# Scatters and gathers from 128 partitions, route steps at two a position late in an item, and register reads item by item

## The chip, the cores and the metric

The kernel runs on one core of a Trainium2 chip. The core has a matrix engine (TensorE, PE in the rows), three engines for elementwise work (VectorE, DVE; ScalarE, ACT; GpSimd, POOL) and a sync engine (SP) that here only issues transfers and reads values into its registers. Each engine takes its instructions in the order of its own program and waits in place for what an instruction needs. The metric is the time of one execution in microseconds, less is better. Before the change the median of three timed runs is 1078.88 us (1070.05 to 1081.38).

## What is computed

Attention with a decaying state, then two layers of experts. The first layer sends a token to one expert, the second to two of eight.

```python
x = attn(q, k, v, a_re, a_im)                  # 3072 tokens x 384
e_idx = argmax(x @ w_gate + modality_bias)     # layer 1: one expert of 8
out[mask] = gate_w * (relu(x[mask] @ w1[e]) @ w2[e])
noisy = x @ w_gate + log1p(exp(x @ w_noise)) * noise
top2 = argpartition(-noisy, 2)[:, :2]          # layer 2: two experts of 8
out[mask] += top2_w * (relu(x[mask] @ w1[e]) @ w2[e])
```

## The kernel before

Attention runs first, by a planner's order, and writes its rows `x1` to HBM. Both expert layers then work in *items*. An item is one block of a token list for one expert: 3 blocks of 122 tokens in layer 1 (`CUT1`; items 6 and 9 are small, one block), 4 blocks of 99 in layer 2 (`CUT2`). Layer 1 has 10 items that always run, layer 2 has 16; more run only behind a branch (`singles`) that tests a count, and in this execution none of them did.

An item (`experts`) is 8 groups of 9 matmuls into `ph` and 3 groups of 24 into `po`, each product in three passes for precision (high by high, high by low, low by high). After each of these 11 groups there is a *position*, p = 0 to 10, at which side work is written into the program: splits of the next item's weights (`w1h`, `w1l` at 7, 7, 8; `w2h`, `w2l` at 0, 2, 3, 5), transposes of the next item's gathered rows `xg` into `xh`, `xl` (`turn`, at 8, 8, 9), the rest of the item before (`fin`, at 0 to 3), and one step of the *route*.

The route (`route2`) turns the noise gates of two or three finished layer-1 items into entries of the second list. It is a generator of nine steps: six of a chain of small VectorE operations up to the mask `mbf`, one in which nothing is done, one in which PE counts ranks (`pr`, matmuls of `ones` and `before` with `pb` and `mbf`; the tile shows as `pt`) and VectorE starts on the slots, and one that ends the `slot` and issues 12 or 14 scatters of `ent` into `list2` on POOL, one for each block and choice. It is set going at p = 3, so that its steps stand at p = 4 to 10 and then at p = 0 and 1 of the next item. There are four routes: in items 2, 4 and 7 of layer 1, and in item 0 of layer 2.

For the second layer, `lead_blocks` loads three list blocks (`lt0` to `lt2`) on POOL's queue once the third route's scatters have landed; `gather2` then gathers the rows `x2` into `xg`, and `prior2` gathers what `out` holds so far into `op`; `out` is scattered back at an item's end (`out_dram<-og`). Weights are loaded into a ring of four buffers `raw` on SP's queue (`load1`, `load2`). Expert numbers and list positions lie in a table (`tb`, or `tbl` for the first three), and the engine that issues a transfer reads them with a value load (TENSOR_LOAD). `load1` and `load2` each read the expert, `block` reads the position. A scheduler places instructions as early as their inputs allow, so value loads come together where a table is ready.

## Time and profile before

| | |
|---|---|
| median of three timed runs | 1078.88 us |
| time of the profiled execution | 1068.24 us |
| its span, first to last instruction | 1066.6 us |
| PE busy | 952.2 us, 89% |
| DVE, ACT, POOL busy | 684.9, 543.3, 550.9 us |
| mean granted TensorE clock | 0.96 of full |

The page gives the busy time of each engine, and the span in 40 slices. A timeline row is a start, a duration, the engine, the line and the operation with its tiles, written `out<-in`; in brackets stands how long the engine was idle before it, and the name of what ended the wait. Most instructions are recorded by one helper and so have its line (L394); they are told apart by tiles. Attention takes the first 308 us, layer 1 runs to 572 us, layer 2 to the end.

### The profile page before, as it was taken

Reading aid. Unit: us, or ns where it says so; the run is one execution under the profiler, and the core shown is the slowest. Engines: PE = TensorE matmul, PEld = TensorE weight load, DVE = VectorE, ACT = ScalarE, POOL = GpSimd, SP = SyncE. Lnnn points to the kernel's source line nnn. Section 1 sums busy time; section 2 is a strip of 40 time slices with the busy share of each in tenths; the row PEclk is TensorE's granted clock in tenths of the full one; section 3 lists DMA queues with packets and bytes.
Section 4 is the critical chain, followed back from the end, with each engine's and each line's share of the span. In section 5 each row is a group of like instructions: output and inputs, shape, how many; then the busy total and the mean of one; then the engine's idle time right before and its main releaser. Section 6 shows DMA issues by size and latency. Waiting matters only on the chain.

```text
span 1066.6 us, 18507 instructions
## 1 busy us (share of the span) xinstructions
PE 952.2 (89%) x6330; PEld 902.7 (85%) x6330; DVE 684.9 (64%) x1504; ACT 543.3 (51%) x990; POOL 550.9 (52%) x449
## 2 busy tenths in 40 slices
PE   2597979889899999999967898899999999999993
PEld 1476767778789999999957798899999999999993
DVE  7599999888767585858844663555555555555540
ACT  7587768777354454456543242444444444444430
POOL 4475766565544237281466386555555444445331
PEclk9898999999999999999987898999999999999997
DMA  6475766531464656577575255665555555565420
GB/s 163 119 202 131 191 177 153 130 118 39 127 166 126 191 150 146 155 188 204 132 179 156 52 99 169 214 186 168 172 166 176 181 177 174 181 186 178 138 75 26
DMA packets 119340, 161.55 MB, mean 151 GB/s; under 512 B 39820, under 2 KB 102091, under 8 KB 119226
## 3 DMA queue, kind: packets, MB, share of 16 engines
q1 hardware_dynamic: 95258, 126.57, 40.4%
q0 software_dynamic: 23968, 33.61, 12.7%
q8 instruction: 54, 0.88, 0.4%
q14 instruction: 60, 0.49, 0.2%
HBM read 130.13 MB, written 30.71 MB: 151 GB/s over the span
## 4 chain that ended last, share of the span: by engine, by line
PE 58%; DVE 11%; issue 10%; DMA 8%; SPq 4%; POOL 4%; ACT 3%; POOLq 0%; DVEq 0%; ACTq 0%
PE po L394 24%; PE ph L394 23%; PE pt L394 5%; SPq L394 2%; POOL list L836 2%; DMA xg<-x,lt 2%; DMA im<-in_a_im_dram 1%; DMA list<-ent,slot 1%; DMA raw<-in_moe_w_dram 1%; PE pp L394 1%; DVE S L394 1%; PE py L394 1%; DVE im L394 1%; PE ptr L394 1%; PE pc L394 1%
## 5 line engine op out<-in xcount | busy, mean ns | idle before, releaser
L394 PE MATMUL ph<-xh,w1h 128*128 128x396 f32 (+1 forms) x576 | 204.7, 355 | 8.9 <-DVE og L869 4.5
L437 POOL DMA_INDIRECT xg<-x,lt x90 | 118.7, 1319 | 175.5 <-DMA lt<-list 64.2
L394 PE MATMUL po<-hh,w2h 128*128 128x396 f32 (+1 forms) x576 | 199.8, 347 | 5.1 <-ACT oT L608 5.1
L394 PE MATMUL ph<-xl,w1h 128*128 128x396 f32 (+1 forms) x576 | 196.7, 342 | 0.0
L394 PE MATMUL ph<-xh,w1l 128*128 128x396 f32 (+1 forms) x576 | 196.2, 341 | 0.0
L394 PE MATMUL po<-hh,w2l 128*128 128x396 f32 (+1 forms) x576 | 196.1, 341 | 0.0
L394 PE MATMUL po<-hl,w2h 128*128 128x396 f32 (+1 forms) x576 | 195.7, 340 | 0.0
L593 ACT ACTIVATE hh<-ph 128x396 fp32r<-128x396 f32 (+1 forms) x192 | 94.5, 493 | 167.6 <-PE ph L394 145.1
L595 DVE SCALAR_TENSOR_TENSOR hl<-ph,hh 128x396 fp32r<-128x396 f32 (+1 forms) x192 | 107.3, 559 | 59.8 <-ACT hh L593 54.7
L608 ACT ACTIVATE oT<-po 128x396 f32<-128x396 f32 (+1 forms) x72 | 35.4, 492 | 175.4 <-PE po L394 166.0
L437 POOL DMA_INDIRECT op<-out_dram,lt x64 | 87.3, 1364 | 72.5 <-DMA out_dram<-og,lt 52.1
L836 POOL DMA_INDIRECT list<-ent,slot x52 | 95.9, 1845 | 47.2 <-DVE slot L833 30.4
L394 PEld LDWEIGHTS ph<-xh,w1h 128*128 128x128 f32 x576 | 109.9, 191 | 10.4 <-DVE og L869 4.8
L873 POOL DMA_INDIRECT out_dram<-og,lt x64 | 68.8, 1076 | 93.5 <-DVE og L869 63.6
L394 PEld LDWEIGHTS po<-hh,w2h 128*128 128x128 f32 x576 | 109.0, 189 | 5.6 <-ACT oT L608 5.5
L556 DVE TENSOR_TENSOR w1l<-raw,w1h 128x1024 fp32r<-128x1024 f32 x78 | 92.2, 1218 | 28.6 <-ACT w1h L556 26.6
L394 PEld LDWEIGHTS ph<-xl,w1h 128*128 128x128 f32 x576 | 110.3, 191 | 0.0
L394 PEld LDWEIGHTS ph<-xh,w1l 128*128 128x128 f32 x576 | 109.9, 191 | 0.1
L394 PEld LDWEIGHTS po<-hl,w2h 128*128 128x128 f32 x576 | 109.3, 190 | 0.0
L394 PEld LDWEIGHTS po<-hh,w2l 128*128 128x128 f32 x576 | 108.8, 189 | 0.0
L869 DVE SCALAR_TENSOR_TENSOR og<-pt,lt,op 99x384 f32<-99x384 f32 x64 | 39.1, 617 | 107.7 <-PE pt L394 71.4
L556 DVE TENSOR_TENSOR w2l<-raw,w2h 128x768 fp32r<-128x768 f32 x104 | 98.9, 951 | 11.0 <-ACT w2h L556 9.3
(341 smaller groups left out, 1810.8 us busy)
## 6 DMA issues: line engine op xcount, KB each, us to landing
raw<-in_moe_w_dram SPq DMA_DIRECT2D x78, 512.0 KB
raw<-in_moe_w_dram SPq DMA_DIRECT2D x104, 384.0 KB
x<-zero SPq DMA_DIRECT2D x12, 457.5 KB
re<-in_a_re_dram SPq DMA_DIRECT2D x24, 192.0 KB
q<-in_q_dram SPq DMA_DIRECT2D x24, 192.0 KB
im<-in_a_im_dram SPq DMA_DIRECT2D x24, 192.0 KB
k<-in_k_dram SPq DMA_DIRECT2D x24, 192.0 KB
v<-in_v_dram SPq DMA_DIRECT2D x24, 192.0 KB
```

The source lines that it names most:

```text
L394: o = f(*a, **kw)
L437: nc.gpsimd.indirect_dma_start(out=dst, out_offset=None, in_=src, in_offset=bass.IndirectOffsetOnAxis(ap=idx, axis=0), bounds_check=n - 1, ...
L556: a, b = nc.scalar.activation(h, r, AF.Copy), nc.vector.tensor_sub(l_, r, h.bitcast(FT))
L593: relu = nc.scalar.activation(a, p, AF.Relu)
L595: rest = nc.vector.scalar_tensor_tensor(l, p, 0.0, a.bitcast(FT), op0=OP.max, op1=OP.subtract)
L608: nc.scalar.activation(oT[:, d, :], p, AF.Copy)
L836: nc.gpsimd.indirect_dma_start(out=list2_v[2 * b + j], out_offset=bass.IndirectOffsetOnAxis(ap=slot[:, j, b:b + 1], axis=0), in_=ent[:, j, ...
L869: nc.vector.scalar_tensor_tensor(og[:, b, :], p, gate[:, b:b + 1], opv[:, b, :], op0=OP.mult, op1=OP.add)
L873: nc.gpsimd.indirect_dma_start(out=out_v[b], out_offset=bass.IndirectOffsetOnAxis(ap=lt[:, b, 1:2], axis=0), in_=og[:, b, :], in_offset=No ...
```

## The change

Tiles that POOL scatters from or gathers into get 128 partitions in place of 122, with the last six set once at the start: `lts`, `lt1s` and `slots` to an index out of bounds, `ents` to zero. The scatters of the second list and the gathers of layer 1 then name all 128 partitions. `new_side` puts two route steps at p = 8, 9 and 10. An expert number is read once for an item, and value loads on SP are queued behind the last `w1` load issued before them.

```diff
-    xgs = [consts.tile([TB_, NB_, XW], FT, name=f"xg{i}") for i in range(2)]
-    lts = [consts.tile([TB_, NB_, 4], I32, name=f"lt{i}") for i in range(K)]
+    xgs = [consts.tile([128, NB_, XW], FT, name=f"xg{i}") for i in range(2)]
+    lts = [consts.tile([128, NB_, 4], I32, name=f"lt{i}") for i in range(K)]
+    lt1s = [consts.tile([128, CUT1.NB, 3], I32, name=f"lu{i}") for i in range(4)]
+    slots = [consts.tile([128, 2, MR], I32, name=f"slot2{i}") for i in range(3)]
+    ents = [consts.tile([128, 2, MR, 4], I32, name=f"ent2{i}") for i in range(3)]
+    for t_ in lts + lt1s + slots:
+        nc.gpsimd.memset(t_, BIG)
+    for t_ in ents:
+        nc.gpsimd.memset(t_, 0)
...
+    def read(x, n, q_=nc.sync):
+        if q_ is nc.sync and loaded and any(i is loaded[-1] for i in nc.cur_bb.bb.instructions):
+            with tc.issue_after(loaded[-1]):
+                return q_.value_load(x, min_val=0, max_val=n)
+        return q_.value_load(x, min_val=0, max_val=n)
+    loaded = []
+
     def block(lt, r, l, cut, q_=nc.sync):
-        r = q_.value_load(r, min_val=0, max_val=(E + 1) * cut.CAP - cut.T)
+        r = read(r, (E + 1) * cut.CAP - cut.T, q_)
...
     def load1(e, w1_):
-        e = nc.sync.value_load(e, min_val=0, max_val=E - 1)
...
-            nc.sync.dma_start(r, w1_[bass.ds(e, 1), d * 128:(d + 1) * 128, :].rearrange("o p f -> p (o f)"))
+            a = nc.sync.dma_start(r, w1_[bass.ds(e, 1), d * 128:(d + 1) * 128, :].rearrange("o p f -> p (o f)"))
             split(side, r, wts[0][:, d, :], wts[1][:, d, :])
+        loaded[:] = [a.ins]
...
     def load2(e, w2_):
-        e = nc.sync.value_load(e, min_val=0, max_val=E - 1)
...
-        e = (first or tb[1])[:, 0, i:i + 1]
+        e = read((first or tb[1])[:, 0, i:i + 1], E - 1)
...
-                gather(xg[:cut.TB, b, :], x1, lt[:cut.TB, b, 0:1], N)
+                gather(xg[:, b, :], x1, lt[:, b, 0:1], N)
...
-        ahead1[i] = wk.tile([CUT1.TB, CUT1.NB, 3], I32, name="lt1", bufs=6)
+        ahead1[i] = lt1s[i % len(lt1s)]
...
-                    out=list2_v[2 * b + j], out_offset=bass.IndirectOffsetOnAxis(ap=slot[:, j, b:b + 1], axis=0),
-                    in_=ent[:, j, b, :], in_offset=None, bounds_check=E * CUT2.CAP - 1, oob_is_err=False)
+                    out=list2_v[2 * b + j], out_offset=bass.IndirectOffsetOnAxis(ap=slots[turn_][:, j, b:b + 1], axis=0),
+                    in_=ents[turn_][:, j, b, :], in_offset=None, bounds_check=E * CUT2.CAP - 1, oob_is_err=False)
...
-                    gather(xgs[i][:CUT1.TB, b, :], x1[:n], lts[i][:CUT1.TB, b, 0:1], n)
+                    gather(xgs[i][:, b, :], x1[:n], lts[i][:, b, 0:1], n)
...
     def new_side():
-        return {p: [step] for p in range(11)}
+        return {p: [step] * (1 + (p >= 8)) for p in range(11)}
```

How the instructions of three engines stand before and after the change follows. On PE, the first rows are those of the third route before the change, where the rank matmuls follow the first `ph` group of item 8:

```order
L394 MATMUL ph<-xh,w1h 128x366
L394 MATMUL ph<-xl,w1h 128x366
L394 MATMUL ph<-xh,w1l 128x366
L394 LDWEIGHTS ones
L394 MATMUL pt<-pb,ones 122x56
L394 LDWEIGHTS before
L394 MATMUL pt<-mbf,before 122x56
```

After the change the same matmuls follow the last `po` matmul of the second group of 24 in item 7:

```order
L402 MATMUL po<-hh,w2l 128x366
L402 LDWEIGHTS ones
L402 MATMUL pt<-pb,ones 122x56
L402 LDWEIGHTS before
L402 MATMUL pt<-mbf,before 122x56
```

They have moved from behind p = 0 of the next item to p = 9 of the item itself, that is by the third `po` group (24 matmuls), the third `turn` and one `ph` group, ahead of all of these; the other three routes move alike. VectorE's rows ahead of `mbf` are the same as before, but for the last `xl` of the item and three small copies, which now stand behind it.

On POOL, the rows after the 14 scatters of the third route, before the change (`lt0` is the list block of item 0 of layer 2, `xg0` takes its rows, `op0` what `out` holds):

```order
L434 ISA
L434 DMA lt0_134<-list2_63 99x4x4
L434 ISA
L434 DMA lt1_135<-list2_63 99x4x4
L433 TENSOR_LOAD tbl2_6641
L433 ISA x2
L434 ISA
L434 DMA lt2_136<-list2_63 99x4x4
L437 DMA xg0_132<-x2_61,lt0_134 99x384 x4
L437 DMA xg1_133<-x2_61,lt1_135 99x384 x3
L437 DMA op0_7069<-out_0_dram,lt0_134 99x384 x4
```

And after the change:

```order
L450 DMA lt0_134<-list2_63 99x4x4
L453 DMA op0_6989<-out_0_dram,lt0_134 99x384
L445 TENSOR_LOAD tbl2_6570
L445 ISA x2
L450 ISA
L450 DMA lt1_135<-list2_63 99x4x4
L453 DMA op0_6989<-out_0_dram,lt0_134 99x384 x2
L445 TENSOR_LOAD tbl2_6570
L445 ISA x2
L450 ISA
L450 DMA lt2_136<-list2_63 99x4x4
L453 DMA xg0_132<-x2_61,lt0_134 99x384 x4
```

Three of the four gathers of `out` have moved ahead of the gathers of `x2`, between the three block loads.

On SP, around the second list block that it loads in layer 2 (item 2), before the change:

```order
L549 DMA raw<-in_moe_w_dram 128x2x384
L434 ISA
L434 DMA lt_12118<-list_63 99x4x4
L433 TENSOR_LOAD tb
L433 ISA x2
L536 TENSOR_LOAD tb
L536 ISA x2
L545 TENSOR_LOAD tb
L545 ISA x2
```

Of such value loads 23 stand there, down to the next weight load (`L540 DMA raw`). After the change:

```order
L564 DMA raw<-in_moe_w_dram 128x2x384
L450 ISA
L450 DMA lt_11889<-list_63 99x4x4
L555 ISA
L555 DMA raw<-in_moe_w_dram 128x1024
```

The weight load follows the block at once; two value loads stand behind the third `w1` load of each item instead.

## Rows read from the trace of the kernel before

**Rows 1.** Page, busy time, share of the span and instructions by engine

```profile
PE 952.2 (89%) x6330; PEld 902.7 (85%) x6330; DVE 684.9 (64%) x1504; ACT 543.3 (51%) x990; POOL 550.9 (52%) x449
```

**Rows 2.** Waits of PE, 400 to 1066 us: total us, times, longest

```profile
PE pt L394 <- DMA xg<-x,lt: 14.8, 4, 11.9
```

**Rows 3.** Timeline of PE at its holes: start, us, operation, idle before

```profile
302.16 0.32 PE L394 MATMUL pt<-ident,xg 122*128 122x122 f32 x1 [1.92 <-DMA xg<-x,lt]
...
550.02 0.33 PE L394 MATMUL po<-w2l,hh 128*122 128x384 f32 x1
562.25 0.40 PE L394 MATMUL pt<-ident,xg 99*128 99x99 f32 x1 [11.90 <-DMA xg<-x,lt]
...
572.26 0.43 PE L394 MATMUL ph<-xh,w1h 128*128 128x396 f32 x1
...
607.77 0.67 PE L394 MATMUL ph<-xh,w1h 128*128 128x396 f32 x1 [4.34 <-DVEq L912]
...
648.05 0.70 PE L394 MATMUL ph<-xh,w1h 128*128 128x396 f32 x1 [4.54 <-DVE og L869]
...
673.70 0.70 PE L394 MATMUL po<-hh,w2h 128*128 128x396 f32 x1 [4.82 <-ACT oT L608]
```

**Rows 4.** Timeline of POOL, 518 to 643 us

```profile
518.55 1.69 POOL L836 DMA_INDIRECT list<-ent,slot  x1 [28.77 <-DVE slot L833]
...
547.63 1.67 POOL L836 DMA_INDIRECT list<-ent,slot  x1 [0.30 <-issue]
553.33 1.73 POOL L434 DMA_DIRECT2D lt<-list  x2 [4.03 <-DMA list<-ent,slot]
...
559.01 1.11 POOL L437 DMA_INDIRECT xg<-x,lt  x1 [2.94 <-DMA raw<-in_moe_w_dram]
...
642.53 1.09 POOL L437 DMA_INDIRECT op<-out_dram,lt  x1 [3.98 <-issue]
```

**Rows 5.** Instructions of tiles `list` and `lt`: ns min/median/max, first and last start

```profile
L836 POOL DMA_INDIRECT list<-ent,slot x52: 1662/1668/4197, 395.5 to 633.0; - x52
L394 POOL DMA_INDIRECT list<-ent,slot x24: 963/1022/2500, 101.0 to 325.6; - x24
...
L873 POOL DMA_INDIRECT out_dram<-og,lt x64: 984/1003/1857, 603.1 to 1054.2; - x64
```

**Rows 6.** Timelines of PE and DVE in routes 1, 3 and 4

```profile
385.26 0.48 PE L394 MATMUL pt<-ident,xg 122*128 122x122 f32 x3
388.64 0.21 DVE L797 TENSOR_TENSOR mbf<-t,vd 122x48 bf16<-122x48 f32 x1
...
508.27 0.48 PE L394 MATMUL pt<-ident,xg 122*128 122x122 f32 x3
512.07 0.22 DVE L797 TENSOR_TENSOR mbf<-t,vd 122x56 bf16<-122x56 f32 x1
...
595.79 0.50 PE L394 MATMUL pt<-ident,xg 99*128 99x99 f32 x4
598.32 0.22 DVE L797 TENSOR_TENSOR mbf<-t,vd 122x56 bf16<-122x56 f32 x1
```

**Rows 7.** A gap of PE in attention, and its windows: us, PE busy, PEclk, DMA share, GB/s

```profile
219.20 1.65 PE L394 MATMUL pp<-qT,kT 96*128 96x128 f32 x8 [3.44 <-DVE pm L394]
...
216.00:220.00 4.00, 0.80 (x6) 0.96 0.35 105
220.00:224.00 4.00, 4.00 (x20) 0.61 0.30 93
```

**Rows 8.** Timeline of SP's queue in layer 2

```profile
647.11 0.36 SPq L434 DMA_DIRECT2D lt<-list  x1
661.41 6.24 SPq L540 DMA_DIRECT2D raw<-in_moe_w_dram  x3
...
712.31 6.17 SPq L540 DMA_DIRECT2D raw<-in_moe_w_dram  x3
721.65 6.37 SPq L549 DMA_DIRECT2D raw<-in_moe_w_dram  x4
```

## The prediction

> **What bounds the kernel now.** I read the page first: PE is busy 89% of the span [rows 1], so time comes or goes where PE stands still or runs at half clock. Next the waits of PE behind 400 us: one entry, the transposes of `xg` waiting for a gather, holds 14.8 us [rows 2]. Then PE's timeline, to see each hole with its ends [rows 3], and the timelines of POOL, DVE and SP at the same times, to see what the hole waits for. The holes are few. From 680 us to the end PE runs item after item without one, so nothing that the change does there can be earned.

> Hole A, 550.4 to 572.3 us: PE stops in item 9 because the first rows of layer 2 are not there. Behind it stand POOL's 14 scatters, 518.55 to 549.3 us, then their landing, the block loads at 553.33 and the gather at 559.01 [rows 4]. The stretch lasts 21.9 us and holds some 4 us of work at full clock (12 matmuls at 0.17, 15 transposes at about 0.1), so it loses about 18. Hole B, before 648.05: 4.54 us, since DVE's `og` waits for the gathers of `out`, which stood behind the fourth route's scatters and began at 642.53 [rows 3, 4]; PE then runs at half clock for 4.8 us, losing 2 more: 6.5. Hole C, before 673.70: 4.82 us plus 1.4 of half clock, 6.2. There ACT waits for `w1`, which SP issued at 661.41; the list block before it was issued at 647.11, and between them SP does 23 value loads, 13.9 us, 0.6 each [rows 3, 8]. The hole before 607.77 is the branch and stays [rows 3]. In front, PE waits 1.92 us for the first gathers [rows 3].

> **The scatters and gathers.** The trace has no scatter from 128 partitions with a bounds check. From 122 partitions one takes 1.67 us, from 99 (with a check) 1.00, from 128 (layer 1's list, 12 byte entries, without a check) 0.96 to 1.02 [rows 5]. The new one is the third kind with the check of the second, so I take 1.00; with the gap of 0.30 that each row shows, 14 take 18.2 us where they now take 30.7 [rows 4]. Bounds: 0.96, and 1.84 on the line through 99 and 122 partitions. The layer 1 gathers are not waited for, except the first (1.92 us, between nothing and all of it saved; I take all).

> [...]

> **The doubled steps.** The nine steps end at p = 10 and not at p = 1 of the next item. But the rank matmuls move to p = 9, and there PE is early. DVE is busy without a gap up to `mbf`, and its order ahead of `mbf` hardly changes: only `xl` and small copies leave, which shortens the chain of dependent operations (0.24 each) by 0.36 in routes 1 to 3, and not in route 4, where `xl` already stood behind. So `mbf` ends, with 0.15 to reach PE, at 388.64, 512.1 and 598.7, and PE stands at that place at 385.26, 508.27 and 595.79 [rows 6]. PE waits 3.4, 3.8 and 2.9 us, and 3.4 again in route 2, which repeats route 1 at 440.6: 13.5 us, all on the path. Below it cannot be: nothing makes DVE faster.

> [...] The four waits lie nearest to that row: 4 x 1.7 = 6.8, with nothing as the lower bound. Together 20.3 us lost.

> In return the slot is early. In route 3 the matmuls start at 512.1; slots need some 2.7 us from there, since the splits and `hl` that stood between are gone. Scatters start at 514.8, not 518.55.

> **Hole A after the change.** 514.8 + 18.2 = 533.0, less the last gap 532.7. Landing 4.0 [rows 4]: `lt0` at 536.7. From that issue to the first gather it now takes 5.7: 542.4. Here the new order counts: a gather of `out` (1.09 + 0.30), a block load (about 1.5 with its value load), two more gathers of `out`, another load, and only then `xg`: 7.1 us, so 549.5. Four gathers at 1.38, and 3.2 from issue to PE (559.01 to 562.25): all four blocks at 556.8. PE comes to the place 3.8 + 1.7 later than now, at 555.9. About 1.5 us stay; 16.4 are saved. What hid the block loads is gone then: every further us on POOL is a us of PE.

> **Holes B and C.** Route 4's slot comes at about 601 us, 14 scatters end at 619.5, `out` is scattered to 625, lands by 629, and the gathers of `out` run then, not at 642.53, while PE needs `og` at about 648. B goes, 6.5. SP's list load, which waits for the same scatters, comes before 630; the 23 value loads are gone, and `w1` follows the ring of buffers, as in later items. C goes, 6.2. The added cost: two value loads behind the third `w1` of every item, 1.2 us. SP idles from 718.5 to 721.65 there now [rows 8], so they are hidden; without that cover, 1.2 us for each of 13 items. The 13 memsets at the start are small and POOL waits for its first attention tile anyway.

> **Sum.** 1.9 + 16.4 + 6.5 + 6.2 = 31.0 saved, 20.3 lost: 10.7 us less. The profiled execution took 1068.24 us, so 1057.5 on its own scale, 1.0% less. The median of the three runs, 1078.88, lies 1% above that execution; the same share off the median gives 1068.

> **Rivals.**
> *PE does not wait at p = 9.* Then 31 us are saved: 1037 on the profiled scale, 1048 on the median's. For it: the edit doubles the steps to have them ready. Against: DVE has no idle time there to be early in. 0.10.
> *The first hole stays in good part*, because the gathers of `out` in front of `xg` are dearer than 1.4 us each, or wait for `lt0` longer. With 8 us more there the saving is 3: 1065, or 1076. For it: the order puts three of them and two block loads in between. 0.17.
> *128 partitions are no cheaper*, the cost growing with rows: 1.84 us, with today's stragglers 2.36 a scatter, 14 take 33 us from 514.8 on, 548; the gathers of `out` then use up the us gained against 549.3. Nothing of A is saved, 14.6 stand against 20.3, and the kernel is slower by 5.7: 1074, or 1085. It decides from about 2.06 us a scatter with its gap. Against: the row at 0.96 to 1.02 is from 128 partitions. 0.13.

> **How the numbers follow.** The forecast, a saving of 7 to 18 (18 where the clock stays up), has 0.57; some 10.8 us are 1%, which is about what a measurement of this kernel can tell from no change, so 0.36 of it is faster and 0.21 the same. With the rivals (0.10 faster; 0.17 the same; of 0.13 half slower by over 1%, since B may stay too) and 0.03 left for the unforeseen: faster 0.47, the same 0.45, slower 0.08. The range goes from 1051 (18 saved, on the profiled scale) to 1080 (nothing saved, on the median's); outside are the rival without waits and the one without cheaper scatters.

> **What would show it.** Right: `list<-ent,slot` near 1.0 us; four new PE waits of about 3 us at the matmul of `mbf`, named after DVE, each with a stretch at half clock behind it; `xg` of layer 2 first issued near 549; no PE wait near 648 and 674; no pile of value loads on SP. The prediction is wrong if the waits at `mbf` are missing or above 5 us, if hole A keeps more than 6 us, or if a new hole stands in the second layer, where I expect none.

## The result: 0.9% slower, and the profile after

The changed kernel takes 1083.93 us (median of 20 runs, 1078.36 to 1090.8), the kernel before 1075.33 in the same runs (20, 1068.13 to 1081.38): a ratio of 1.0088 with a 95% interval of [1.0067, 1.011]. The forecast was 1068 us, a gain of 1%, with a range of 1051 to 1080. The profiled execution took 1084.25 us, its span is 1082.6 us (before 1066.6). So the two profiles lie 16.0 us apart and the medians 8.6: the profiled execution of the kernel before, 1068.24 us, lies at the fast end of its range. Times and ratios in this document leave out executions in a second, slower state; of the kernels below only g122_again has any (5 of 10, its profile among them).

The page of the changed kernel, busy time of two engines (us, share of the span, instructions):

```profile
PE 961.9 (89%) x6330; PEld 910.6 (84%) x6330; DVE 685.6 (63%) x1504; ACT 543.7 (50%) x990; POOL 497.4 (46%) x462
```

POOL has 53 us less to do than before, and PE still is busy 89% of a span that is now 16 us longer [rows 1]. The list scatters cost what was forecast; instructions of the tile `list`, ns min/median/max:

```profile
L853 POOL DMA_INDIRECT list<-ent,slot x52: 982/983/1597, 398.3 to 643.0; - x52
```

They take 0.98 us in place of 1.67 [rows 5]. Waits of PE from 300 us to the end (us in total, times, longest):

```profile
PE ph L402 <- DVE hl L610: 14.2, 5, 9.5
PE ph L402 <- issue: 12.7, 3, 4.8
PE pt L402 <- DVE mbf L812: 10.2, 4, 3.2
PE ph L402 <- DVEq L929: 4.0, 1, 4.0
```

The same view of the kernel before, from 300 us to the end ([rows 2] has its stretch from 400 us on):

```profile
PE pt L394 <- DMA xg<-x,lt: 16.7, 5, 11.9
PE po L394 <- ACT oT L608: 5.1, 2, 4.8
PE ph L394 <- DVE og L869: 4.5, 1, 4.5
```

The 16.7 us for `xg` are gone, and so are the 4.5 for `og` and the 4.8 before 673.7. The four waits for `mbf` are there, 10.2 us. The branch stays, 4.0. But the two first lines of the changed kernel are new, 26.9 us at the first product of an item (`ph`), and nothing in the forecast speaks of them. They are the loss.

By stages, cut at three PE rows (first `ph` of item 0, first transposes of layer 2's `xg`, first `ph` behind the branch), the time from one to the next. The third line is a kernel of the experiments below, the changed one with layer 1's gathers from 122 partitions:

| kernel | to item 0 | item 0 to layer 2 | to the branch | to the end of the span |
|---|---|---|---|---|
| before | 308.7 | 253.6 | 45.5 | 458.8 |
| changed | 315.1 | 279.5 | 40.3 | 447.7 |
| gathers from 122 | 315.7 | 254.6 | 42.1 | 445.0 |

The second half came out as hoped: 11 us less behind the branch, 5 before it. The first half, where the forecast has 16.4 saved against some 16 lost, takes 26 us more.

The longest of the new holes, rows from the timelines of PE, ACT, DVE and POOL (start, us, operation, idle before it and what ended it):

```profile
477.90 0.33 PE L402 MATMUL ph<-xh,w1l 128*128 128x366 f32 x1
487.72 0.67 PE L402 MATMUL ph<-xh,w1h 128*128 128x366 f32 x1 [9.48 <-DVE hl L610]
...
478.12 0.58 ACT L734 ACTIVATE og<-pt,lu 122x384 f32<-122x384 f32 x1 [2.38 <-PE ph L402]
486.62 0.48 ACT L608 ACTIVATE hh<-ph 128x366 fp32r<-128x366 f32 x1 [7.92 <-remote]
...
487.12 0.54 DVE L610 SCALAR_TENSOR_TENSOR hl<-ph,hh 128x366 fp32r<-128x366 f32 x1 [7.87 <-ACT hh L608]
...
473.13 0.98 POOL L853 DMA_INDIRECT list<-ent,slot  x1 [0.30 <-issue]
480.85 0.98 POOL L853 DMA_INDIRECT list<-ent,slot  x1 [0.30 <-issue]
483.50 1.02 POOL L453 DMA_INDIRECT xg<-x,lu  x1 [0.30 <-issue]
```

Read it backwards. PE waits for `hl`, `hl` waits for `hh`, and `hh` on ACT waits 7.92 us for "remote". What `hh` needs is `ph`, and by its records PE ended the last three groups of `ph` at 475.22, 476.73 and 478.23. "Remote" is what the profile writes where a semaphore update ended the wait and no instruction ends near that update. There is no other core here. The updates of PE's semaphore themselves tell more (the trace holds them, no view prints them). At 468.93 us a group ends and its update is recorded 0.014 us later, as nearly everywhere (0.014 us is the median of this trace, and 94% of the recorded updates lie within 0.03 us behind the end of a matmul that makes one). From 470.7 on the updates fall behind, first by 0.06 and 0.09 us. The signals due at 473.71, 475.22, 476.73 and 478.23 are the last four before the hole. The last four updates are recorded at 478.10, 486.59, 486.70 and 486.80, the last three 0.1 us apart, as if let go at once. **PE's work was done, its signal came 4 to 11 us later.** I call this a late signal. All through it POOL issues 128-partition transfers 1.29 us apart, from 466.34 us on. The DMA engines are not full: from 466 to 490 us they were busy for 0.35 of the time and moved 93 GB/s, in the kernel before 0.80 and 193 GB/s in that stretch.

The same pattern stands at the end of the other three runs of scatters and of the run of six `xg` gathers and four scatters at 285 to 298 us. In sum, waits of ACT from 300 us on, in the changed kernel and in the kernel before:

```profile
ACT hh L608 <- remote: 26.5, 5, 7.9
```

```profile
ACT hh L593 <- remote: 0.9, 1, 0.9
```

The kernel before is not quite free of it: a dozen of its updates come 1 to 3 us late, the latest near 664 us beside scatters and gathers from 99 partitions 1.3 to 1.4 us apart, but ACT waits 0.9 us for one of them, and no hole of [rows 3] stands behind one.

### The profile page after: what moved, and what is told of

Its sections match the earlier page's. It is cut to its first block, busy times and chain, and to the rows that moved or that the text cites. A ratio compares the mean times of both kernels' runs of the same rounds, so it can differ in the third digit from the quotient of the medians.

```text
span 1082.6 us, 18445 instructions
## 1 busy us (share of the span) xinstructions
PE 961.9 (89%) x6330; PEld 910.6 (84%) x6330; DVE 685.6 (63%) x1504; ACT 543.7 (50%) x990; POOL 497.4 (46%) x462
## 5 line engine op out<-in xcount | busy, mean ns | idle before, releaser
L402 PE MATMUL ph<-xh,w1h 128*128 128x396 f32 (+1 forms) x576 | 207.1, 360 | 31.0 <-DVE hl L610 14.2
L402 PE MATMUL ph<-xh,w1l 128*128 128x396 f32 (+1 forms) x576 | 198.7, 345 | 0.0
L453 POOL DMA_INDIRECT xg<-x,lt x73 | 81.1, 1110 | 115.7 <-DMA lt<-list 66.6
L453 POOL DMA_INDIRECT op<-out_dram,lt x64 | 92.0, 1438 | 74.3 <-DMA out_dram<-og,lt 52.5
L587 DVE TENSOR_TENSOR xl<-pt,xh 128x396 fp32r<-128x396 f32 (+2 forms) x78 | 39.8, 533 | 77.1 <-ACT xh L586 72.8
```

The lines of the kernel that those rows point to most:

```text
L402: o = f(*a, **kw)
L453: nc.gpsimd.indirect_dma_start(out=dst, out_offset=None, in_=src, in_offset=bass.IndirectOffsetOnAxis(ap=idx, axis=0), bounds_check=n - 1, ...
L587: done.append(nc.vector.tensor_sub(xl[:, d, :], p, xh[:, d, :].bitcast(FT)))
```

## The experiments

It turned out to matter on which chip a kernel ran, so the kernels are told in the groups that shared a chip, with the kernel before on that chip. Each chip was used in one series of measurements, so what goes with the chip here could as well go with the series; the chip of the first result is not on record.

| kernel | chip | us | before | ratio, 95% interval | late signals |
|---|---|---|---|---|---|
| s122 | 12 | 1071.9 | 1074.8 | 0.9959 [0.9913, 1.0006] | none |
| g122 | 12 | 1057.1 | 1074.8 | 0.9854 [0.9799, 0.991] | none |
| single_steps | 12 | 1041.4 | 1074.8 | 0.9684 [0.9654, 0.9715] | none |
| paced | 12 | 1057.3 | 1074.8 | 0.9828 [0.9793, 0.9863] | none |
| after_again | 8 | 1080.3 | 1075.5 | 1.0038 [1.0013, 1.0064] | yes |
| only128 | 8 | 1060.5 | 1075.5 | 0.9856 [0.9812, 0.9899] | yes |
| only_doubled | 8 | 1084.9 | 1075.5 | 1.0081 [1.0055, 1.0106] | few |
| only_read | 8 | 1068.1 | 1075.5 | 0.9928 [0.9895, 0.9961] | few |
| after_third | 6 | 1081.4 | 1079.2 | 1.0030 [0.9993, 1.0067] | yes |
| single_again | 6 | 1057.2 | 1079.2 | 0.9831 [0.9766, 0.9896] | yes |
| g122_again | 6 | 1078.2 | 1079.2 | 1.0004 [0.9962, 1.0047] | yes |
| after_fourth | 7 | 1085.8 | 1080.8 | 1.0056 [1.0033, 1.0079] | yes |
| single124 | 7 | 1055.0 | 1080.8 | 0.9777 [0.9728, 0.9826] | few |
| paced_again | 7 | 1097.0 | 1080.8 | 1.0145 [1.0102, 1.0187] | yes |
| doubled124 | 4 | 1062.8 | 1074.6 | 0.9886 [0.9847, 0.9926] | none |
| spaced | 4 | 1057.4 | 1074.6 | 0.9846 [0.9801, 0.9891] | none |

("None" is no update of PE's semaphore over 1 us late outside the end of the program, "few" is none that stops PE for over 2.5 us. Two more, bursts on chip 6 and bursts2 on chip 7, carry extra transfers that make them longer, 1148.6 and 1135.0 us, and are read by their traces alone.)

**On chip 12: one part of the change taken back each time.** Theory 1 was that 128-partition transfers in long runs make the signals late, theory 2 that the doubled steps collide with the items' work, theory 3 that the value reads hold up the weights.

s122, scatters from 122 partitions again:

```diff
-  ap=slots[turn_][:, j, b:b + 1], ... in_=ents[turn_][:, j, b, :]
+  ap=slots[turn_][:TB, j, b:b + 1], ... in_=ents[turn_][:TB, j, b, :]
```

> The changed kernel with the list2 scatters from 122 partitions again; the layer 1 gathers stay at 128, the steps doubled, the values read item by item. Theory 1 (signals): in the changed kernel TensorE's semaphore updates reach ScalarE late during a long run of POOL transfers from 128 partitions, and the new TensorE holes near 415, 420, 488, 564, 648 and 653 us (25.8 us, and half clock behind them) come from that. Then these holes are gone here, no ACT wait at hh named remote is above 1 us, the scatters take 1.67 us again, hole A before the xg transposes of layer 2 is back with 10 to 18 us, the hole near the end of the attention part (6.2 us) stays, and the time is about 1075 us (0.99 of the changed kernel, 1.00 of the kernel before). Theory 2 (steps): the doubled steps put route work where it collides with ScalarE's and VectorE's item work; then the holes stay, hole A comes on top, and the time is 1095 to 1105. Theory 3 (values): the value reads behind the third w1 load make the weights late; then the holes stay as in theory 2.

g122, layer 1's gathers from 122 again:

```diff
-  gather(xg[:, b, :], x1, lt[:, b, 0:1], N)
+  gather(xg[:cut.TB, b, :], x1, lt[:cut.TB, b, 0:1], N)
-  gather(xgs[i][:, b, :], x1[:n], lts[i][:, b, 0:1], n)
+  gather(xgs[i][:CUT1.TB, b, :], x1[:n], lts[i][:CUT1.TB, b, 0:1], n)
```

> The changed kernel with the layer 1 gathers from 122 partitions again; list2 scatters stay at 128. Theory 1 (signals): at the end of the attention part the 6 gathers and 4 scatters no longer run back to back at 1.3 us, so the hole of 6.2 us at 297.6 us is gone; the runs of 12 and 14 scatters are as before, so at least three of the later holes stay. Time about 1077 us, 0.993 of the changed kernel. Theory 2 (steps) and theory 3 (values): the hole at 297.6 us is unexplained by them and all holes stay; the time is that of the changed kernel, 1084, or more by what dearer gathers (1.72 for 1.0 us) delay.

single_steps:

```diff
-  return {p: [step] * (1 + (p >= 8)) for p in range(11)}
+  return {p: [step] for p in range(11)}
```

> The changed kernel with one route step per place, as in the kernel before; 128 partitions and values item by item stay. Both theories: the four waits for mbf (10.2 us, and up to 6.8 of half clock) go. Theory 1 (signals): the runs of 128-partition scatters still stand there, only later against the items, so ACT waits at hh named remote and holes of together 15 to 30 us stay; hole A keeps 0 to 5 us; time 1066 to 1074. Theory 2 (steps): no new hole is left, and what 128 partitions save (31 us less 2) shows in full: about 1045 to 1052. Theory 3 (values): the holes stay, as in theory 1.

paced, a memset behind each scatter:

```diff
+  idle = consts.tile([128, 576], FT, name="idle")
   nc.gpsimd.indirect_dma_start(out=list2_v[2 * b + j], ...)
+  nc.gpsimd.memset(idle, 0.0)
```

> The changed kernel with a POOL memset of 128 x 576 fp32 (estimated 0.5 to 0.7 us by the row of the 99 x 1536 memset at 1.39) behind each list2 scatter, so that 128-partition scatters start about every 1.9 us, as those from 122 partitions did, and not every 1.28. Theory 1 in the form that the pace counts (a backlog that drains at a fixed rate): the holes near 415 to 653 us are gone or under 2 us in sum, hole A is back in good part, time about 1075. Theory 1 in the form that each such transfer holds the signals, whatever the pace: the holes stay or grow, and hole A is added: 1090 to 1105. Theories 2 and 3: the holes stay as well.

Three of the four were much better than theory 1 allows (g122 1057.1 for some 1077, single_steps 1041.4 for 1066 to 1074, paced 1057.3 for 1075 or more). s122 alone is near it, 1071.9 for 1075, with hole A back at 11.1 us, but without the hole at the end of the attention part that theory 1 left there. None of the four has a hole behind `hl` above 2 us. PE's waits from 300 us on, in g122 and then in single_steps:

```profile
PE pt L402 <- DVE mbf L812: 10.2, 4, 3.2
PE ph L402 <- DVEq L929: 4.1, 1, 4.1
...
PE pt L402 <- DMA xg<-x,lt: 1.6, 1, 1.6
```

```profile
PE pt L402 <- DMA xg<-x,lt: 8.7, 4, 3.9
PE ph L402 <- DVEq L929: 4.3, 1, 4.3
```

single_steps has runs of 14 scatters from 128 partitions 1.29 us apart, and no late signal; theory 1 as I wrote it seemed to fall, and theory 2 to hold (1045 to 1052 expected, 1041 measured). paced tested nothing of what it was meant for: the memsets depend on nothing, the scheduler had put them at the front of the program (the first eight from 6.54 us), and the scatters stood 1.29 us apart as ever. With hindsight it is the changed kernel with 52 memsets at the front.

**On chip 8: the changed kernel again, and one part alone each time.** The three others are the kernel before with one part of the change and without the others.

> The changed kernel itself, beside three that each have one part of the change. In the four runs so far no TensorE hole behind hl above 2 us is left, also where the runs of 14 scatters from 128 partitions stand with 1.28 us from start to start (one step per place, 1041.4 us; gathers from 122, 1057.1 us). So theory 1 in its plain form is too wide. Theory 1b (together): late signals need the doubled steps, 128-partition gathers and 128-partition scatters all at once: the time is 1080 to 1088 again, with ACT waits at hh of 4 to 8 us named remote. Theory 4 (condition): the late signals belong to the execution conditions of the first measurement, not to the kernel: the time here is about 1057, as for the kernel with gathers from 122, and no such wait is there.

> The kernel before with 128 partitions alone (scatters and layer 1 gathers), one step per place, old value loads. By my sum 128 partitions save 1.9 + about 12 of hole A (scatters 518.55 + 18.2 = 536.7, so the xg gather 551 and not 559) + 6.5 of hole B = 20: 1055. If the pile of value loads is what holds w1 back (hole C, 6.2), that hole stays here. Theory 1b: no late signals. A theory that 128-partition transfers alone make the signals late: 1075 or more with ACT waits named remote.

> The kernel before with the doubled steps alone. By my sum: four TensorE waits for mbf, 13.5 us by the prediction and 10.2 by the changed kernel's trace, with up to 6.8 of half clock, less 3.7 of hole A since the third route's scatters start earlier: plus 12 to 17, 1087 to 1092. Rival (the clock does not fall): plus 7, 1082. Theory 2 (collision with item work): holes at hl or hh as in the changed kernel, 1100 or more.

> The kernel before with values read item by item alone. By my sum hole C (6.2 us before 673.7) goes, and nothing else: 1069. Rival: the two reads behind the third w1 load of each item are on the path, 1.2 us for each of some 25 items: 1095 or more. Rival: the pile was hidden, no change, 1075.

The changed kernel is slow again, with its late signals. But only128 has them as well, with one step per place, so theory 2 falls: PE waits 7.0 us for `hh`, the first row here, and single_steps, which differs from it in the value reads alone, had waited for nothing of the kind.

```profile
PE po L402 <- ACT hh L609: 7.0, 2, 4.1
```

What differed between the two groups was the chip. PE's waits in only_doubled, then in only_read:

```profile
PE pt L394 <- DMA xg<-x,lt: 14.2, 5, 10.6
PE pt L394 <- DVE mbf L797: 9.8, 4, 3.1
PE po L394 <- ACT oT L608: 4.6, 1, 4.6
```

```profile
PE pt L394 <- DMA xg<-x,lt: 16.4, 5, 12.2
PE ph L394 <- DVE hl L601: 4.7, 3, 4.0
```

The doubled steps alone cost 9.5 us (12 to 17 expected). The value reads alone save 7.3 (6.2 expected): hole C, `po` waiting for `oT` (4.82 us in [rows 3]), is gone; hole B stays, 4.0 us, and nothing stands for the two reads of each item. The 128 partitions alone save 15.0, with the late signals in.

**On chip 6: does it go with the chip?** Theory 4 says that the late signals go with the conditions of a series, such as its chip; theory 1b that only the three parts together make them.

> The changed kernel once more, beside the two of the first four whose traces had no late signals. What is open: the kernels measured on one chip (scatters from 122, gathers from 122, single steps, paced) show no late signal, those measured on another (the changed kernel, 128 alone) show them. Theory 4 (condition): lateness goes with the chip on which a kernel runs, so here all kernels of this call show it or none: either 1055 to 1060 for this kernel and no ACT wait at hh named remote above 1 us, or 1078 to 1085 with such waits. Theory 1b (together): this kernel 1078 to 1085 with waits, the next two without.

> 128 partitions and values item by item, one step per place, again (1041.4 us before). Theory 4: where the changed kernel shows late signals in this call, so does this one, with 15 to 25 us of TensorE holes behind hl and hh, and a time of 1053 to 1063; where it does not, 1041. Theory 1b: 1041 whatever the changed kernel shows.

> The changed kernel with the layer 1 gathers from 122 partitions, again (1057.1 us before). Theory 4: where the changed kernel shows late signals here, this one shows them in the runs of 12 and 14 scatters, and takes 1072 to 1080; where it does not, 1057. Theory 1b: 1057.

single_again is word for word single_steps. It took 1041.4 us on chip 12 (kernel before 1074.8) and 1057.2 on chip 6 (1079.2); g122 went from 0.985 of the kernel before to 1.000. Theory 1b falls, theory 4 stands: on chip 6 all three have late signals. (The changed kernel itself was never run on a chip without them, and its ratio on chip 6, 1.0030, can't be told from 1.) PE's waits in single_again:

```profile
PE ph L402 <- issue: 5.2, 1, 5.2
PE po L402 <- ACT hh L608: 4.6, 1, 4.6
PE ph L402 <- DVEq L929: 4.3, 1, 4.3
```

> The kernel before with five runs of 14 extra POOL scatters of 16 byte rows into memory of their own, put at the front of items 4, 6, 8, 10 and 12 of layer 2, where the kernel has no long run: from 128, 122, 126 and 124 partitions, and from 128 with every row out of bounds. They compute nothing that is used. [...] Theory B (only 128 is cheap): 124 and 126 stay at 1.6. Where this call shows late signals: theory 1 wants waits of ACT at hh named remote in item 4 (128), none in item 6 (122); if out of bounds rows count as well, in item 12 too. POOL's own work is late by 4 to 15 us in these items, so the time is 10 to 60 us above before and is not compared.

bursts adds, to the kernel before, transfers that belong to nothing:

```diff
+  for j in range(k * 14, (k + 1) * 14):
+      nc.gpsimd.indirect_dma_start(out=dump_v[j],
+          out_offset=bass.IndirectOffsetOnAxis(ap=(big if at else spot)[:n, j:j + 1], axis=0),
+          in_=junk[:n, :], in_offset=None, bounds_check=5 * 14 * 128 - 1, oob_is_err=False)
```

They depended on nothing either and ran at the front of the program, 6 to 126 us. There PE was busy 31 of the 112 us in which they ran (five windows), and no signal was late by over 0.5 us, on the chip on which the three kernels above have late ones. But the price is clean. Steady rows from 128, 122, 126 and 124 partitions, then from 128 with all rows out of bounds:

```profile
16.93 0.97 POOL L392 DMA_INDIRECT dump<-junk,spot  x1 [0.30 <-issue]
...
46.83 1.67 POOL L392 DMA_INDIRECT dump<-junk,spot  x1 [0.30 <-issue]
...
68.68 0.99 POOL L392 DMA_INDIRECT dump<-junk,spot  x1 [0.30 <-issue]
...
89.07 1.31 POOL L392 DMA_INDIRECT dump<-junk,spot  x1 [0.30 <-issue]
...
120.86 0.98 POOL L392 DMA_INDIRECT dump<-junk,big  x1 [0.30 <-issue]
```

So 124 partitions cost 1.31 us and 126 cost 0.99: it isn't a matter of 128. What sets these steps no run shows.

**On chip 7: the transfers by themselves.** Theory 5 says that the pace counts, that is into how many parts a transfer goes, divided by the time from one transfer to the next. The number of parts was the author's assumption and no run shows it; only the time between transfers is measured. bursts2 holds six runs of 12 such transfers in their places, behind the gathers of `op` in items 3, 5, 7, 9, 11 and 13 of layer 2, while PE runs the experts:

```diff
+  BURST = {3: (0, 128, 0), 5: (1, 122, 0), 7: (2, 126, 0), 9: (3, 124, 0), 11: (4, 128, 1), 13: (5, 128, 2)}
+      o = nc.gpsimd.indirect_dma_start(out=dump_v[j], ...)
+      after(o, last)
```

(1 in the last place: all rows out of bounds; 2: a memset behind each, held by the same kind of dependency.)

> The kernel before with six runs of 12 extra POOL scatters of 16 byte rows into memory of their own, held in place behind the gathers of op in items 3, 5, 7, 9, 11 and 13 of layer 2, while TensorE runs the experts: from 128, 122, 126 and 124 partitions, from 128 with every row out of bounds, and from 128 with a memset of 128 x 576 behind each. They compute nothing that is used. Prices by the runs at the front of the last kernel: 0.97, 1.67, 0.99, 1.31, 0.97. [...] POOL's own gathers are late by up to 15 us behind the run of 122, so the time is not compared.

Windows of 29 us from the start of each run, in that order: busy time of PE, PEld, DVE, ACT, POOL with instruction counts, then granted clock, DMA share, GB/s:

```profile
713.00:742.00 29.00, 18.61 (x98) 17.55 (x97) 6.71 (x12) 5.48 (x10) 20.01 (x21) 0.83 0.33 80
783.00:812.00 29.00, 29.00 (x173) 28.85 (x172) 15.25 (x22) 12.46 (x21) 24.27 (x16) 1.00 0.65 113
846.00:875.00 29.00, 15.75 (x78) 14.72 (x77) 5.33 (x10) 5.09 (x9) 20.03 (x20) 0.78 0.30 72
917.00:946.00 29.00, 29.00 (x173) 28.86 (x172) 15.25 (x22) 12.46 (x21) 23.82 (x18) 1.00 0.55 124
984.00:1013.00 29.00, 13.79 (x66) 12.88 (x65) 7.12 (x12) 3.96 (x7) 20.73 (x21) 0.69 0.33 101
1051.00:1080.00 29.00, 29.00 (x173) 28.86 (x172) 15.84 (x24) 12.50 (x22) 24.34 (x29) 1.00 0.52 138
```

This is the clearest table of the study, though each line is one run of transfers in one execution. PE stays busy for all of 29 us behind transfers from 122 partitions, from 124, and from 128 spaced 1.74 us apart. It loses 10 to 15 us behind those from 128 (1.29 us apart), 126 (1.29) and 128 with every row out of bounds (1.29). So it needs neither data nor the list, nor 128 as such. A pace as in theory 5 would fit, but so does a simpler rival that needs no number of parts: the time between two transfers alone. All three bad runs have 1.29 us from start to start, the good ones 1.97 (122), 1.61 or more (124) and 1.74 (128, spaced), and no run has 122 or 124 partitions at 1.29. The longest waits of ACT at `hh` in the three bad windows:

```profile
735.70 0.50 ACT L615 ACTIVATE hh<-ph 128x396 fp32r<-128x396 f32 x1 [10.85 <-remote]
...
870.63 0.50 ACT L615 ACTIVATE hh<-ph 128x396 fp32r<-128x396 f32 x1 [10.81 <-remote]
...
1010.04 0.50 ACT L615 ACTIVATE hh<-ph 128x396 fp32r<-128x396 f32 x1 [15.04 <-remote]
```

One thing was not swapped: the bad runs stand in items 3, 7 and 11, the good ones in 5, 9 and 13. The kernel before has no hole of PE in any of these items, but no run excludes that the place counts too.

single124 is single_steps with 124 in place of 128 for scatters and gathers; after_fourth is the changed kernel; paced_again is paced.

> One step per place, values item by item, scatters and layer 1 gathers from 124 partitions. Price of a scatter 1.31 + 0.30, so 14 take 22.5 us (18.2 from 128, 30.7 from 122 and stragglers). Theory 5: no late signals on any chip. Hole A is some 4 us longer than with 128 on a chip without late signals (1041 + 4 = 1045), holes B and C stay away. On a chip with late signals 1045 as well, where 128 partitions gave 1057. Rival: late signals come here too, 1055 or more.

> The changed kernel with a memset behind each scatter, on a chip that may show late signals (1057.3 us on the chip without). [...] Rival (each transfer from 128 partitions holds the signals, whatever the pace): holes as in the changed kernel, 1075 or more.

> The changed kernel in the same call. Theory 4: if the traces of this call show late signals, 1078 to 1085; if not, about 1057, which is what the prediction's sum gave on the profiled scale (1057.5).

single124 on a chip with late signals has no PE wait for them above 2.5 us; what stays is hole A:

```profile
PE pt L402 <- DMA xg<-x,lt: 9.2, 3, 8.3
PE ph L402 <- DVEq L929: 4.3, 1, 4.3
PE ph L402 <- issue: 2.6, 2, 2.4
```

It is 2.2% faster than the kernel before, against 1.7% for single_again on chip 6. Its time, 1055, is 10 above what I expected; the kernel before takes 6 more here than on chip 12, hole A with 9.2 is not longer than in single_steps (8.7), and the rest I can't account for. The time alone, 1055, would also fit the rival, which gave 1055 or more. The trace decides against it only in part: signals do come up to 5.8 us late (near 570 and 676 us), but beside gathers and scatters from 99 partitions 1.3 to 1.4 us apart, and the longest stop of PE there is 2.4 us. So theory 5's "no late signals on any chip" is wrong as it stands; what is gone with 124 partitions, 1.61 us apart, is the long holes at the route's scatters. paced_again has the holes of the changed kernel, since its memsets are at the front here as well; it takes 11 us more than after_fourth, and item 0 starts 11 us later in it. It says nothing about pace.

**On chip 4: the same cures in the changed kernel itself**, that is the changed kernel with scatters and layer 1 gathers from 124 partitions in place of 128 (doubled124), and with scatters spaced by memsets that are held in place (spaced):

```diff
+  if b or j:
+      after(o, rest_)
+  rest_ = nc.gpsimd.memset(idle, 0.0)
+  after(rest_, o)
```

> [...] A scatter takes 1.31 and a gap of 0.30, so 14 take 22.5 us and not 18.2. Theory 5 (the pace of engine parts): no late signals on any chip, so the forecast of the prediction holds up to the dearer scatters: 1057.5 on the profiled scale and 4 to 8 us more in hole A, 1062 to 1066; on the median's scale 1062 to 1075. In the chain of waits: four waits for mbf of 10 us in sum, no TensorE hole behind hl above 2.5 us. Rival (the doubled steps make the collision): holes as in the changed kernel, 1080 or more.

> The changed kernel with a POOL memset of 128 x 576 (0.60 us) behind each list2 scatter, held in its place by an order dependency. In the two runs of the paced kernel the memsets had been moved to the front of the program and the scatters still stood 1.29 us apart, so they tested nothing of pace. Here they start 1.75 us apart, as in item 13 of the bursts, where TensorE stayed busy for all of 29 us. 14 take 24.5 us. Theory 5: on a chip with late signals no TensorE hole behind hl above 2.5 us near the scatters (one at the end of the attention part, where gathers and scatters still follow at 1.3 us, stays); hole A 4 to 8 us; 1065 to 1075. Rival (128 partitions as such, or the number of transfers in all, not the pace): holes of 3 to 7 us stay, 1085 or more.

Both times are as expected or better, and no signal is late by over 1 us. But chip 4 behaves like chip 12: in spaced the gathers and scatters at the end of the attention part still follow one another at 1.3 us, and the hole that theory 5 leaves there on a chip with late signals (6.2 us in the changed kernel) is missing. So neither kernel can tell theory 5 from its rivals. What they show is the forecast's sum with dearer or slower scatters; PE's waits in spaced, where a scatter starts every 1.74 us:

```profile
PE pt L404 <- DVE mbf L814: 10.1, 4, 3.2
PE pt L404 <- DMA xg<-x,lt: 9.0, 2, 7.7
PE ph L404 <- PEq L935: 5.1, 1, 5.1
```

## Why the prediction was wrong

**The step that failed** is in "The scatters and gathers". It priced a 128-partition transfer by the time that POOL spends on it, 1.00 us, and put into the sum nothing for what such transfers do to other engines. The nearest rows had been little warning: the transfers from 128 partitions in the kernel before [rows 5] come in fours, in the attention part, and the late updates that its trace holds stopped PE nowhere. Of the signs named for being wrong it was the last, "a new hole ... where I expect none", that came, though four of the five runs of late signals stand ahead of the second layer, and one in it (the holes before 648.11, in the place of the old hole B, and before 652.88). In the profiled execution the new holes at `ph` are 26.9 us, and the granted clock is 0.50 to 0.63 in the 3.2 us behind five of the six longest. On the profiled scale the forecast had 10.7 us saved and 16.0 were lost, a miss of 26.7 us. That this is so near to 26.9 is in part chance: the other terms were off by some us in both directions. On chip 12 these holes are in none of the three kernels that have long runs of 128-partition transfers beside a busy PE; on chips 6, 7 and 8 they are in all eight that have such runs.

**The rest of the mechanism came as forecast where no signal was late.** g122 on chip 12 shows it best: the four waits for `mbf` are there, hole A is gone but for 1.6 us, and holes B and C are gone. It saves 17.7 us by the medians and 9.1 between the profiled executions (1068.24 and 1059.11, from two series), where 10.7 were forecast, 8.8 of them without the front's 1.9. So the sign and the rough size are confirmed, the sum to the microsecond is not. Step by step:

- Scatter 1.00 us: 0.98.
- Hole A, 16.4 saved and 1.5 left: 1.6 us of `xg` waits are left in g122, none in the changed kernel, where PE comes later. That the gathers of `out` and the block loads would stand in front of `xg` was right: in the changed kernel the third route's last scatter ends at 564.68, `lt0` is issued at 566.66 and the first `xg` at 577.75, 13.1 us after the scatter; the forecast had 16.8 (532.7 to 549.5).
- Holes B and C, 12.7 saved: both are gone in g122 and in the changed kernel. only_read shows that the value reads alone take away C, and only128 that earlier scatters alone do so too: no w1 hole stands there. The two are not additive.
- Waits at p = 9, 13.5 us: 10.2 in five kernels (3.19, 3.22, 2.52 and 1.26 in the changed one). Forecast were 3.4, 3.4, 3.8 and 2.9, so routes 3 and 4 were sized too large. From the end of `mbf` to PE's start it took 0.05 us in the changed kernel, where 0.15 was reckoned.
- Half clock, 6.8 us: 6.3. g122's windows of 3.2 us behind the four waits:

```profile
395.00:398.20 3.20, 3.20 (x16) 3.20 (x16) 2.28 (x18) 0.48 (x1) 0.00 (x0) 0.50 0.03 5
398.20:401.40 3.20, 3.20 (x14) 3.20 (x12) 0.00 (x0) 0.00 (x0) 2.50 (x2) 0.55 0.06 4
455.90:459.10 3.20, 3.18 (x16) 3.17 (x16) 2.27 (x18) 0.48 (x1) 0.00 (x0) 0.50 0.00 0
527.10:530.30 3.20, 3.18 (x17) 3.18 (x17) 2.39 (x19) 0.48 (x1) 0.07 (x1) 0.54 0.02 5
530.30:533.50 3.20, 3.20 (x19) 3.20 (x19) 0.00 (x0) 0.00 (x0) 2.59 (x3) 0.93 0.02 1
600.80:604.00 3.20, 3.20 (x25) 3.20 (x25) 2.19 (x16) 0.51 (x1) 0.51 (x1) 1.00 0.00 0
```

  The missing shares are 0.50, 0.45, 0.50, 0.46 and 0.07, 1.98 windows of 3.2 us. The wait of 1.24 us cost no clock, those of 2.5 us and more did. In the profiled execution of the changed kernel itself only the first of its waits did (0.77 and 0.70, 1.7 us). The forecast's 1.7 us for one wait is what the two windows of [rows 7] miss of the full clock, and the trace of the kernel before has the granted clock at 0.50 from 219.7 to 223.1 us, 3.4 us. That each of the four waits would cost as much, no run shows: they cost 6.3 us together in g122 and 1.7 in the changed kernel.
- Value reads hidden: yes, only_read is faster.
- The front, 1.9 saved: the `xg` wait is gone, but in the changed kernel a late signal stops PE for 6.2 us at 297.6; item 0 starts 6.5 us later than before, at 315.1. But g122, without late signals and with the old gathers, starts it at 315.7, s122 and single_steps, with the new gathers on the same chip, at 306.9 and 308.5, and only_read, with the old front, at 314.6. The start moves by more than 1.9 us without the change, so what the front gained is not settled.

**The rivals.** That the doubled steps would not cost anything had 0.10 and is refuted (only_doubled, 9.5 us). That 128 partitions would not be cheaper had 0.13, and is refuted (0.98 us). That the first hole stays had 0.17, and is refuted with scatters of 0.98 us (1.6 us left in g122). The case that happened was not among them: it had at most the 0.03 for the unforeseen. The doubled steps are the part that should have been doubted more: the forecast itself had them at 20.3 us against 3.7 us by which they bring the third slot forward, and the better kernel, single_steps, is the one without them, 0.968 of the kernel before on chip 12 and 0.983 on chip 6.

**What stays open.** Why the signals come late. The traces with late signals have another mark: in them 8 to 12% of the updates of PE's semaphore have no record (840 of 923 in the changed kernel), while on chips 12 and 4 nearly all have one (924 updates for 923 instructions in g122, two of them after the program's last). The loss of records does not come from the change: the kernel before has 841 for 920 in its profile, and only_read on chip 8, with old scatters and gathers, 839 for 920. Each of the timed executions here was recorded, since each lists its span and clock. So it can be that recording itself is what holds up the signal where records also get lost, and that an execution without recording would show the forecast's time on every chip; it can also be that both have a common cause in the traffic. No run here tells the two apart. Nor is it shown inside the kernel that spacing alone or 124 partitions alone cure the changed kernel on a chip with late signals: doubled124 and spaced ran on a chip without them. That rests on bursts2 and, for the 124 partitions, single124, and neither tells whether it is the 124 partitions or the longer time between transfers that does it. Chip and series were never told apart either.

## What to carry to other kernels

Price a POOL transfer by what it does to the other engines too: one from 126 or 128 partitions is cheap for POOL (0.97 to 0.99 us), but a dozen in a row, 1.29 us apart, beside a busy TensorE made TensorE's signals late, by 4 to 11 us in the profile of the changed kernel, and again in three of five series; in bursts2, which has 126 as well, PE lost 10 to 15 of 29 us. Where a profile says that a wait ended by "remote" on a single core, look at the semaphore's own updates before blaming an engine. And measure a change in more than one series, on more than one chip, and part by part: here three parts together were 0.9% slower, while two of them were 1.7 to 3.2% faster.
